# Gate and value products of a gated MLP as seven block products for each eight, with weight parts decoded early into DRAM

## The chip, the cores and the metric

One core of a Trainium2 chip runs the program. The metric is the device time of one execution in microseconds; lower is better. TensorE does the matrix products, VectorE (DVE in the rows), ScalarE (ACT) and GpSimd (POOL) the work on elements, and SyncE (SP) issues the DMAs.

## The reference

Three layers follow each other. The first is a linear attention with decay over 4 batches, 8 heads, 768 positions, in chunks of 32. Its output, 3072 tokens of 256, goes through an MLP with a cosine, and that through a gated MLP:

```python
h = x @ w_in
g = h * np.cos(h)
x = (g @ w_out).astype(np.float32)                  # d_ff 2048

gate = 1.0 / (1.0 + np.exp(-(x @ w_gate)))
val = x @ w_val
return (gate * val @ w_out).astype(np.float32)      # d_ff 1536, w_gate drawn 8 times larger
```

The weights arrive as 64-bit floats and are decoded on the chip.

## The kernel before, in words

Tokens are worked in NJ = 6 blocks j of 512 (128 positions of each of the 4 batches), held in `x2` with the 256 features as two halves of 128 partitions. Hidden units are worked in blocks f of 128: 16 in the cosine MLP, 12 in the gated one. Every product is made from split operands, a high part (`hi`, a rounded copy) and a low part (the rest): high x high, low weight x high data, high weight x low data.

The attention (`add_att`) and the cosine MLP (`add_mlp1`) of different blocks overlap. `add_conv1` decodes the cosine MLP's weights. When the last attention block is done, `open_later` gives its SBUF to the gated MLP's buffers, and `add_conv2` decodes that MLP's weights, one f at a time: three loads of 64-bit words (L323), then four instructions that make a 32-bit float in `wk` (L336 or L338 rebase, L343 shift, L347 low word, L353 sign), then a high copy (L299) and a low part (L304). They go into two buffers `own` and into the room of the cosine MLP's weights `w1` as that comes free.

The gated MLP (`add_mlp2`) has 72 steps, six blocks j of twelve f. A step has six matmuls of 512 columns for gate and six for value (`hid`, recorded under the helper's line L292), a sigmoid from PSUM on ScalarE (L777), gate times value on VectorE (L779), a high copy of the result (L299 or L301), a low part (L304), and the output product: four matmuls of 512 columns with the result's high part as weights and four of 256 with its low part. `add_split` makes the high and low parts of a block's tokens. Step s's output stands behind step s+1's gate and value products. After f = 11 the four output banks are evacuated (L299, L806) and written by SP (L809).

The order on every engine is fixed when the program is built. `add` records each operation with the engines it may use and their costs, and what it reads and writes; `Order.run` places operations one by one on the engine where each ends first, by due times that `rank` works back from the places (`turn`) that products have on TensorE. The constants in `P` set these (`t0`, `stretch`, `hop`, `slack` and others). `Shared` costs are those that the planner does not let overlap with POOL. So one changed cost or constant moves rows on all engines.

Of the kernel before, what the change touches and what calls it, by code (L numbers as in the profile page):

```python
# [8 lines left out]
F32 = mybir.dt.float32  # L9
# [21 lines left out]
    t0=30000,  # L31
    stretch=(1.2, 1.0),
    hop=500,
    gap=50,
    late=100,
    dlat=2500,
    slack=50,
    hid=-2.4,
    op1=1.3,
# [155 lines left out]
def linear_attention__then__cos_mlp__then__gated_mlp_kernel(  # L195
# [70 lines left out]
    r_t = ring(const, 2, [128, TOK], F32, "r")  # L266
    sq_t = ring(const, 2, [128, TOK], F32, "sq")
    gm_t = ring(const, 2, [128, TOK], F32, "gm")
    gh_t = ring(const, 2, [128, TOK], F32R, "gh")
    gl_t = ring(const, 2, [128, TOK], F32R, "gl")  # L270

    a_clip = [dram.tile([NB * H, S], F32, name=f"a_clip{i}") for i in range(2)]
# [38 lines left out]
    def add_conv(fs, srcs, raw, raw_r, wk, wk_r, hi_lo, w_r, extra=()):  # L311
# [13 lines left out]
        for f in fs:  # L325
            for i in range(len(srcs)):
                at = len(rows)
                rows.append(raw_r(at))
                add({"SP": 730}, lambda e, f=f, i=i, at=at: load(f, i, at), w=[rows[at]], r=extra)
# [57 lines left out]
    OWN = 2  # L387

    def w2_at(f):
        if f < OWN:  # L390
            return later["own"][f][:, 0], later["own"][f][:, 1]
        o = (f - OWN) * 768
        return w1[:, 0, o:o + 768], w1[:, 1, o:o + 768]

    def w2_out(f):
        if f < OWN:
            return later["own"][f][:, :, 512:768]
        o = (f - OWN) * 768
        return w1[:, :, o + 512:o + 768]

    def w2_room(f):
        return [("own", f)] if f < OWN else [("w1", 3 * (f - OWN) + i) for i in range(3)]

    NR = 4

    def add_conv2(f):
        add_conv(
            (f,), w2_src, lambda: later["raw"][f % NR], lambda at: ("raw", f % NR, at), lambda: later["wk"][f % 3],
            ("wk2", f % 3), lambda: w2_at(f), w2_room(f), extra=["later"],
        )  # L410
# [261 lines left out]
    def add_mlp1(s):  # L672
        j, f, first, last, again = steps[s]
        p, hb = xt_room(j), h_bank[s % 3]
        hp, u = bank[hb], s % 2
# [4 lines left out]
        def hid(e):  # L680
# [11 lines left out]
        r, sq, g, gh, gl = r_t[u], sq_t[u], gm_t[u], gh_t[u], gl_t[u]  # L692
        ri = r.bitcast(I32)
        hr = [("bank", hb)]
        add({"ACT": act_b(512) - 40}, lambda e: nc.scalar.activation(  # L695
            out=ri, in_=hp, func=ACTF.Identity, bias=quarter_sb), r=hr + ["round"], w=[("r", u)])
        add({"DVE": dve(512)}, lambda e: nc.vector.tensor_tensor(  # L697
            out=r, in0=ri, in1=hp, op=ALU.subtract), r=hr, w=[("r", u)])
        add({"ACT": act_b(512)}, lambda e: nc.scalar.activation(  # L699
            out=sq, in_=r, func=ACTF.Sin, scale=-TURN, bias=right_sb), r=[("r", u)], w=[("sq", u)])  # L700
        add({"DVE": dve(512)}, lambda e: nc.vector.tensor_tensor(  # L701
            out=g, in0=sq, in1=hp, op=ALU.mult), r=hr + [("sq", u)], w=[("gm", u)])
# [35 lines left out]
    TOTAL1 = NJ * FF1  # L740

    def slot2(s):
        return TOTAL1 + 2 + 1.5 * s

    def add_split(j):
        p = j % 2
        for k in range(KD):
            src, room = x2[:, j, k * TOK:(k + 1) * TOK], [(("x2", j), k)]
            xh = [("xh", p, b, k) for b in range(NB)]
            xl = [("xl", p, b, k) for b in range(NB)]  # L750
            add({"ACT": act(512), "DVE": dve2(512)}, lambda e, k=k, src=src: copy(e, xt_hi[p][:, k], src),
                r=room, w=xh)
            add({"POOL": pool(512), "DVE": dvs(512)},
                lambda e, k=k, src=src: minus(e, xt_lo[p][:, k], src, f32(xt_hi[p][:, k])), r=room + xh, w=xl)

    def add_mlp2(s):
        j, f = divmod(s, FF2)
        p, u = j % 2, s % 2
        gb, vb = gv_bank[s % 2]
        xh = [("xh", p, b, k) for b in range(NB) for k in range(KD)]  # L760
        xl = [("xl", p, b, k) for b in range(NB) for k in range(KD)]
        wh, wl = ([(n, *y) for y in w2_room(f)] for n in ("hi", "lo"))

        def hid(m, o):
            n = 0
            for i, xv in ((0, xt_hi), (1, xt_hi), (0, xt_lo)):
                for k in range(KD):
                    c = m * 256 + k * 128
                    mm(o, w2_at(f)[i][:, c:c + 128], xv[p][:, k], start=(n == 0), stop=(n == 3 * KD - 1))
                    n += 1  # L770

        shared = {5: ["cb"], 6: [("ya", 0), "ds"], 7: ["ct", ("ya", 1), ("turned", 0), ("turned", 1)]}
        for m, bk in enumerate((gb, vb)):
            add({"PE": 1362}, lambda e, m=m, bk=bk: hid(m, bank[bk]),
                r=xh + xl + wh + wl, w=[("bank", bk)] + shared.get(bk, []), turn=(slot2(s - 1) + 0.1 * m, 2))
        sg, g, gh, gl = sq_t[u], gm_t[u], gh_t[u], gl_t[u]
        add({"ACT": act(512)}, lambda e: nc.scalar.activation(  # L777
# [121 lines left out]
```

## Time and profile before

| | us |
|---|---|
| median of 3 runs (660.06 to 661.70) | 661.25 |
| profiled execution | 659.34 |
| span of its trace, first to last instruction | 657.6 |
| TensorE, matmuls busy | 627.8 (95%) |
| VectorE busy | 469.5 (71%) |
| ScalarE busy | 320.7 (49%) |
| POOL busy | 214.5 (33%) |

The span is the profiled execution less 1.74 us around it. Busy is the time in which an engine has an instruction under way; matmuls overlap, so one matmul's record is longer than the distance to the next. A wait stands beside the instruction that ended it.

### The profile page before, as it was taken

Reading aid. Unit: us, or ns where it says so; the run is one execution under the profiler, and the core shown is the slowest. Engines: PE = TensorE matmul, PEld = TensorE weight load, DVE = VectorE, ACT = ScalarE, POOL = GpSimd, SP = SyncE. Lnnn points to the kernel's source line nnn. Section 1 sums busy time; section 2 is a strip of 40 time slices with the busy share of each in tenths; the row PEclk is TensorE's granted clock in tenths of the full one; section 3 lists DMA queues with packets and bytes.
Section 4 is the critical chain, followed back from the end, with each engine's and each line's share of the span. In section 5 each row is a group of like instructions: output and inputs, shape, how many; then the busy total and the mean of one; then the engine's idle time right before and its main releaser. Section 6 shows DMA issues by size and latency. Waiting matters only on the chain.

```text
span 657.6 us, 9670 instructions
## 1 busy us (share of the span) xinstructions
PE 627.8 (95%) x3468; PEld 498.2 (76%) x3468; DVE 469.5 (71%) x810; ACT 320.7 (49%) x568; POOL 214.5 (33%) x206
## 2 busy tenths in 40 slices
PE   3678999999999999999999999999999999999997
PEld 2355688768867867877788888888888888888886
DVE  7999989997998698686889976446446446445444
ACT  3365799758767766754989632112112112112111
POOL 2336777758767557644565000000000000000000
PEclk9999999999999999999999999999999999999999
DMA  8999950566397167123424200000000000000100
GB/s 161 195 218 232 206 119 27 128 120 114 76 177 157 37 119 138 33 40 99 154 90 140 97 0 14 20 0 10 23 1 8 25 1 3 31 1 0 33 1 32
DMA packets 158947, 50.67 MB, mean 77 GB/s; under 512 B 118515, under 2 KB 155219, under 8 KB 158899
## 3 DMA queue, kind: packets, MB, share of 16 engines
q1 hardware_dynamic: 158899, 50.05, 34.1%
q8 instruction: 27, 0.44, 0.3%
q14 instruction: 21, 0.17, 0.1%
HBM read 36.21 MB, written 3.34 MB: 60 GB/s over the span
## 4 chain that ended last, share of the span: by engine, by line
PE 85%; DVE 9%; DMA 2%; issue 2%; SPq 1%; ACT 0%; DVEq 0%
PE bank L292 85%; DVE lt L556 2%; DVE gm L701 1%; DVE g L573 1%; DVE r L697 1%; DMA raw<-in_moe_w_gate_dram 1%; SPq L323 1%; DVE wk L353 1%; DMA bc<-in_B_dram 1%; DMA x<-in_moe_w_out_dram 1%; DVE ee L535 1%; DMA ab<-in_a_dram 1%; DVE wk L343 1%; DVE xt_lo L637 0%; PE bank L532 0%
## 5 line engine op out<-in xcount | busy, mean ns | idle before, releaser
L292 PE MATMUL bank<-xt_hi,w 128*128 128x512 f32 x864 | 236.7, 395 | 2.6 <-DVE gm L701 1.8
L292 PEld LDWEIGHTS bank<-xt_hi,w 128*128 128x128 f32 x864 | 156.9, 189 | 33.7 <-DVE gm L701 2.8
L304 POOL TENSOR_TENSOR gl<-gm,gh 128x512 fp32r<-128x512 f32 x96 | 147.4, 1537 | 97.1 <-ACT gh L299 61.0
L777 ACT ACTIVATE sq<-bank 128x512 f32<-128x512 f32 x72 | 43.1, 598 | 210.6 <-PE bank L292 210.4
L779 DVE TENSOR_TENSOR gm<-sq,bank 128x512 f32<-128x512 f32 x72 | 49.5, 688 | 132.7 <-PE bank L292 131.2
L292 PE MATMUL bank<-xt_lo,w 128*128 128x512 f32 x432 | 133.6, 390 | 0.0
L292 PE MATMUL bank<-gh,w 128*128 128x512 f32 x384 | 107.4, 397 | 0.5 <-DVE x L731 0.5
L292 PEld LDWEIGHTS bank<-xt_lo,w 128*128 128x128 f32 x432 | 81.4, 188 | 17.8 <-DVE xt_lo L637 0.2
L695 ACT ACTIVATE r<-bank,quarter_sb 128x512 int32<-128x512 f32 x96 | 65.5, 683 | 36.9 <-PE bank L292 36.6
L292 PEld LDWEIGHTS bank<-gh,w 128*128 128x128 f32 x384 | 70.1, 188 | 17.3 <-ACT sq L699 1.1
L701 DVE TENSOR_TENSOR gm<-sq,bank 128x512 f32<-128x512 f32 x96 | 65.1, 679 | 24.2 <-ACT sq L699 22.5
L299 ACT ACTIVATE gh<-gm 128x512 fp32r<-128x512 f32 x103 | 64.8, 629 | 24.8 <-DVE gm L701 13.5
L699 ACT ACTIVATE sq<-r,right_sb 128x512 f32<-128x512 f32 x96 | 68.7, 718 | 8.0 <-DVE r L697 7.8
L697 DVE TENSOR_TENSOR r<-r,bank 128x512 f32<-128x512 int32 x96 | 65.0, 679 | 10.3 <-ACT r L695 9.6
L292 PE MATMUL bank<-w,gh 128*128 128x512 f32 x240 | 64.6, 389 | 0.0
L292 PE MATMUL bank<-gl,w 128*128 128x512 f32 x192 | 62.7, 401 | 0.0
L556 DVE TENSOR_TENSOR_SCAN lt<-ab,id_t 128x512 f32<-128x512 f32 x40 | 52.5, 1313 | 0.0
L292 PEld LDWEIGHTS bank<-w,gh 128*128 128x128 f32 x240 | 45.0, 188 | 9.2
L304 DVE TENSOR_TENSOR gl<-gm,gh 128x512 fp32r<-128x512 f32 x72 | 49.7, 691 | 2.1
L292 PEld LDWEIGHTS bank<-w,gl 128*128 128x128 f32 x240 | 36.8, 189 | 4.9 <-DVE gl L304 0.3
L292 PEld LDWEIGHTS bank<-gl,w 128*128 128x128 f32 x192 | 34.5, 188 | 7.4 <-issue 0.2
L292 PE MATMUL bank<-w,gl 128*128 128x256 f32 x240 | 38.7, 282 | 0.0
(98 smaller groups left out, 606.0 us busy)
## 6 DMA issues: line engine op xcount, KB each, us to landing
ab<-a_clip SPq DMA_DIRECT2D x20, 512.0 KB
x<-in_moe_w_in_dram SPq DMA_DIRECT2D x16, 256.0 KB
x<-in_moe_w_out_dram SPq DMA_DIRECT2D x16, 256.0 KB
xs<-in_x_dram SPq DMA_DIRECT2D x24, 128.0 KB
raw<-in_moe_w_gate_dram SPq DMA_DIRECT2D x12, 256.0 KB
raw<-in_moe_w_val_dram SPq DMA_DIRECT2D x12, 256.0 KB
raw<-in_moe_w_out_dram SPq DMA_DIRECT2D x12, 256.0 KB
out_dram<-o SPq DMA_DIRECT2D x24, 128.0 KB
```

Of the source, the lines that this page charges most:

```text
L292: nc.tensor.matmul(out_, lhsT, rhs, start=start, stop=stop, skip_group_check=True)
L299: nc.scalar.activation(out=out_, in_=in_, func=ACTF.Copy)
L304: engine[eng].tensor_tensor(out=out_, in0=in0, in1=in1, op=ALU.subtract)
L323: nc.sync.dma_start(out=dst, in_=src)
L343: nc.vector.tensor_scalar(out=wi, in0=wi, scalar1=3, scalar2=None, op0=ALU.logical_shift_left)
L556: add({"DVE": scan(512) if j else float(scan(512))}, lambda e, hs=hs, src=src: nc.vector.tensor_tensor_scan(out=lt[:, hs].rearrange("p h t ...
L695: add({"ACT": act_b(512) - 40}, lambda e: nc.scalar.activation(out=ri, in_=hp, func=ACTF.Identity, bias=quarter_sb), r=hr + ["round"], w=[ ...
L697: add({"DVE": dve(512)}, lambda e: nc.vector.tensor_tensor(out=r, in0=ri, in1=hp, op=ALU.subtract), r=hr, w=[("r", u)])
L699: add({"ACT": act_b(512)}, lambda e: nc.scalar.activation(out=sq, in_=r, func=ACTF.Sin, scale=-TURN, bias=right_sb), r=[("r", u)], w=[("sq ...
L701: add({"DVE": dve(512)}, lambda e: nc.vector.tensor_tensor(out=g, in0=sq, in1=hp, op=ALU.mult), r=hr + [("sq", u)], w=[("gm", u)])
L777: add({"ACT": act(512)}, lambda e: nc.scalar.activation(out=sg, in_=bank[gb], func=ACTF.Sigmoid), r=[("bank", gb)], w=[("sq", u)])
L779: add({"DVE": dve(512)}, lambda e: nc.vector.tensor_tensor(out=g, in0=sg, in1=bank[vb], op=ALU.mult), r=[("sq", u), ("bank", vb)], w=[("gm ...
```

## The change

Tokens of two blocks j and hidden units of two blocks f now form a pair. Its gate product is a 2 by 2 block matrix (features by hidden units) times a 2 by 2 block matrix (features by tokens), and so is its value product. Eight block products would make it; the change makes it with seven, after Strassen and Winograd. Four of the seven weight blocks are sums or differences (L488 in the new numbering), formed once and kept, so that a weight part has seven blocks; the seven token operands (`add_operands`) are formed once for two j. Four PSUM banks collect the seven products, and what two results share is moved between banks: twice a product set a bank is copied to SBUF on ScalarE (`put`) and added to two banks on VectorE, from PSUM and SBUF into PSUM (`plus`, L938). The sigmoid, the multiplication, the split and the output then run for the four results. The output product is turned to 256 columns throughout.

There are 18 pairs, six for each of three passes over two token blocks. The weights come in 18 parts (six double blocks, for gate, value and output), each of 256 by 256. The first six parts are decoded during the attention, into work buffers of the cosine MLP's decoding, and written to DRAM (`kept`); they are read back when the gated MLP's buffers are opened. The cosine MLP's four rings of intermediate results become one ring of three buffers, used in place.

```diff
 P = dict(
-    t0=30000,
-    stretch=(1.2, 1.0),
-    hop=500,
+    t0=18000,
+    stretch=(1.25, 1.0),
+    hop=700,
...
-    op1=1.3,
+    op1=1.0,
+    both=12,
+    early=6,
...
-    r_t = ring(const, 2, [128, TOK], F32, "r")
-    sq_t = ring(const, 2, [128, TOK], F32, "sq")
...
+    NG = 3
+    gm_t = ring(const, NG, [128, TOK], F32, "gm")
...
+    def add_early(n, p):
+        i = 3 * n + p
+        j = NJ - 1 - (i % 2 if i < P["both"] else 0)
+        wk, wk_r = wk1_t[i % 2][:, 0:512], ("wk1", i % 2)
+        add_decode(n, p, x2[:, j], [(("x2", j), k) for k in range(2)], lambda: wk, wk_r)
+        add({"SP": 700}, lambda e: nc.sync.dma_start(out=kept[i], in_=wk), r=[wk_r], w=[("kept", i)])
+
+    def add_conv2(n, p):
...
+        if i < P["early"]:
+            add({"SP": 700}, lambda e: nc.sync.dma_start(out=wk()[:, 0:512], in_=kept[i]),
+                r=["later", ("kept", i)], w=[wk_r])
+        else:
+            j = i % 2
+            add_decode(n, p, x2[:, j], [(("x2", j), k) for k in range(2)], lambda: wk()[:, 0:512], wk_r, ["later"])
+        if p < 2:
...
+            for o, x0, x1, op in ((4, 0, 2, ALU.add), (5, 4, 1, ALU.subtract), (6, 1, 0, ALU.subtract),
+                                  (7, 3, 5, ALU.subtract)):
+                add({"DVE": dvs(128), "POOL": pool(128)}, lambda e, o=o, x0=x0, x1=x1, op=op: engine[e].tensor_tensor(
+                    out=block(o), in0=block(x0), in1=block(x1), op=op), w=[wk_r])
...
-    def add_mlp2(s):
-        j, f = divmod(s, FF2)
...
+    P6, P1, P5, P2, P3, P7, P4 = (4, 0), (0, 1), (3, 2), (2, 3), (6, 4), (5, 5), (1, 6)
+    own_op = {5: ("xh", 2), 2: ("xl", 2), 0: ("xh", 0), 1: ("xl", 0), 6: ("xh", 1)}
...
+        b11, b12, b21, b22 = half(j0, 0), half(j1, 0), half(j0, 1), half(j1, 1)
...
+        less(tt, b22, b12, rb22 + rb12, t)
+        split(5, tt, t)
+        less(b12, b12, b11, rb11, rb12)
+        split(2, b12, rb12)
...
+    def add_pair(n):
+        jp, fp = divmod(n, NP)
...
+            product(P6, be, True, 0.1)
+            product(P1, al, True, 0.2)
+            put(0, al)
+            plus(de, be, 0)
+            plus(be, be, 0)
+            product(P5, ga, True, 0.3)
+            out_before(2 * m)
+            product(P2, al, False, 1.1)
+            product(P3, de, False, 1.2)
+            product(P7, be, False, 1.3)
+            put(1, ga)
+            plus(de, de, 1)
+            plus(ga, be, 1)
+            out_before(2 * m + 1)
+            product(P4, be, False, 2.1)
```

Each `product` is three matmuls of 512 columns. `be`, `al`, `ga`, `de` are the four banks, which change roles from one product set to the next.

How rows move is shown at three places. TensorE in the last pass, one whole step before; `bank0` to `bank7` are PSUM banks, `xt_hi`/`xt_lo` the tokens' parts, `w1` weights, `gh`/`gl` the results' high and low parts:

```order
L292 MATMUL bank1_67<-xt_hi1_84,w1_82 128x512 x4
L292 MATMUL bank1_67<-xt_lo1_87,w1_82 128x512 x2
L292 MATMUL bank2_68<-xt_hi1_84,w1_82 128x512 x4
L292 MATMUL bank2_68<-xt_lo1_87,w1_82 128x512 x2
L292 MATMUL bank3_69<-w1_82,gh0_95 128x512
L292 MATMUL bank4_70<-w1_82,gh0_95 128x512
L292 MATMUL bank5_71<-w1_82,gh0_95 128x512
L292 MATMUL bank6_72<-w1_82,gh0_95 128x512
L292 MATMUL bank3_69<-w1_82,gl0_97 128x256
L292 MATMUL bank4_70<-w1_82,gl0_97 128x256
L292 MATMUL bank5_71<-w1_82,gl0_97 128x256
L292 MATMUL bank6_72<-w1_82,gl0_97 128x256
```

and now, from the first product set's P1 of a pair to behind its P3 (`xt` and `op` buffers hold the seven token operands; `xt_lo1` holds the fourth result's parts):

```order
L294 MATMUL bank0_66<-xt_lo0_86,w1_82 128x512 x3
L294 MATMUL bank5_71<-xt_hi0_83,w1_82 128x512 x3
L294 MATMUL bank3_69<-w1_82,xt_lo1_87 128x256 x2
L294 MATMUL bank4_70<-w1_82,xt_lo1_87 128x256 x2
L294 MATMUL bank2_68<-xt_lo2_88,w1_82 128x512 x3
L294 MATMUL bank3_69<-w1_82,gh0_92 128x256 x2
L294 MATMUL bank4_70<-w1_82,gh0_92 128x256 x2
L294 MATMUL bank3_69<-w1_82,gh0_92 128x256 x2
L294 MATMUL bank4_70<-w1_82,gh0_92 128x256 x2
L294 MATMUL bank1_67<-op1_2917,w1_82 128x512 x3
L294 MATMUL bank3_69<-w1_82,gl0_95 128x256 x2
L294 MATMUL bank4_70<-w1_82,gl0_95 128x256 x2
```

Products of three and short output runs of four or eight matmuls alternate; the output is that of the pair before.

VectorE where the gated MLP begins, before (`L701` and `L697` belong to the cosine MLP, the others decode):

```order
L347 SCALAR_TENSOR_TENSOR wk20_2852<-raw3_2851,wk20_2852 128x768
L697 TENSOR_TENSOR r1_90<-r1_90,bank1_67 128x512
L353 SCALAR_TENSOR_TENSOR wk20_2852<-raw3_2851,wk20_2852 128x768
L697 TENSOR_TENSOR r0_89<-r0_89,bank2_68 128x512
L701 TENSOR_TENSOR gm1_94<-sq1_92,bank1_67 128x512
L343 TENSOR_SCALAR wk21_2853<-wk21_2853 128x768
L304 TENSOR_TENSOR w1_82<-wk20_2852,w1_82 128x768
```

and now, in its first pass (`L938` are the new additions, `L966` gate times value, `L306` low parts, `L451` a decode):

```order
L938 TENSOR_TENSOR bank5_71<-bank0_66,cp0_2918 128x512
L966 TENSOR_TENSOR gm0_89<-gm0_89,bank1_67 128x512
L938 TENSOR_TENSOR bank0_66<-bank0_66,cp0_2918 128x512
L938 TENSOR_TENSOR bank5_71<-bank5_71,cp1_2919 128x512
L451 SCALAR_TENSOR_TENSOR wk20_2914<-x2_81,wk20_2914 128x512
L966 TENSOR_TENSOR gm1_90<-gm1_90,bank5_71 128x512
L938 TENSOR_TENSOR bank2_68<-bank0_66,cp1_2919 128x512
L306 TENSOR_TENSOR gl0_95<-gm0_89,gh0_92 128x512
L966 TENSOR_TENSOR gm2_91<-gm2_91,bank2_68 128x512
L306 TENSOR_TENSOR gl1_96<-gm1_90,gh1_93 128x512
L966 TENSOR_TENSOR gm3_2920<-gm3_2920,bank0_66 128x512
L306 TENSOR_TENSOR w1_82<-wk21_2915,w1_82 128x896
```

The additions that TensorE's products wait for stand in one queue with decodes and low parts. SP during the attention's last blocks (`stk`, `bc`, `xs`, `ab` are the attention's inputs), now:

```order
L428 DMA x2_81<-in_moe2_w_gate_dram 128x2x256
L465 DMA kept1_144<-wk11_142 128x512
L428 DMA x2_81<-in_moe2_w_out_dram 128x2x256
L465 DMA kept0_143<-wk10_141 128x512
L613 DMA_TRANSPOSE stk1_120<-pk1_116 128x16x128
L513 DMA xs3_104<-in_x_dram 128x8x32
L513 DMA bc0_105<-in_C_dram 128x8x16
```

Before, no weight load and no store stood between the attention's rows there.

## Rows read from the trace of the kernel before

**Rows 1.** The page, busy us, share of the span and count of each engine.

```profile
PE 627.8 (95%) x3468; PEld 498.2 (76%) x3468; DVE 469.5 (71%) x810; ACT 320.7 (49%) x568; POOL 214.5 (33%) x206
```

**Rows 2.** Windows: busy us (count) of PE, PEld, DVE, ACT, POOL; clock, DMA share, GB/s.

```profile
0.00:66.00 66.00, 43.08 (x351) 26.49 (x352) 60.68 (x123) 32.10 (x67) 25.27 (x33) 1.00 0.97 201
...
200.00:306.00 106.00, 105.98 (x677) 80.91 (x670) 84.88 (x157) 72.46 (x126) 60.26 (x56) 1.00 0.39 76
...
356.00:400.00 44.00, 44.00 (x213) 37.05 (x213) 36.14 (x53) 22.38 (x32) 1.63 (x1) 1.00 0.17 55
400.00:640.00 240.00, 240.00 (x1165) 202.38 (x1164) 117.47 (x208) 43.28 (x82) 0.00 (x0) 1.00 0.04 12
```

**Rows 3.** Chain of waits, late part: start us, length us, what.

```profile
308.86 4.30 DMA raw<-in_moe_w_gate_dram
...
318.05 334.48 PE bank L292 x1601
...
652.97 1.47 DVE o L806 x4
```

**Rows 4.** Timeline of TensorE, one gated step: start us, length us, instructions.

```profile
500.44 1.07 PE L292 MATMUL bank<-xt_hi,w 128*128 128x512 f32 x4
501.34 0.62 PE L292 MATMUL bank<-xt_lo,w 128*128 128x512 f32 x2
...
502.70 0.64 PE L292 MATMUL bank<-w,gl 128*128 128x256 f32 x4
503.17 1.09 PE L292 MATMUL bank<-xt_hi,own 128*128 128x512 f32 x4
504.10 0.62 PE L292 MATMUL bank<-xt_lo,own 128*128 128x512 f32 x2
504.56 1.07 PE L292 MATMUL bank<-xt_hi,own 128*128 128x512 f32 x4
```

**Rows 5.** Timeline of VectorE in the same stretch.

```profile
503.01 0.42 DVE L301 CAST gh<-gm 128x512 fp32r<-128x512 f32 x1
503.34 0.68 DVE L304 TENSOR_TENSOR xt_lo<-x,xt_hi 128x512 fp32r<-128x512 f32 x1
503.94 0.68 DVE L304 TENSOR_TENSOR gl<-gm,gh 128x512 fp32r<-128x512 f32 x1
```

**Rows 6.** Groups by line and shape: count, busy us, mean ns, idle before.

```profile
L779 DVE TENSOR_TENSOR gm<-sq,bank 128x512 f32<-128x512 f32 x72 | 49.5, 688 | 132.7 <-PE bank L292 131.2 <-POOL gl L304 1.2 <-ACT wk L336 0.3
L292 PEld LDWEIGHTS bank<-w,gl 128*128 128x128 f32 x240 | 36.8, 189 | 4.9 <-DVE gl L304 0.3
L301 DVE CAST gh<-gm 128x512 fp32r<-128x512 f32 x65 | 27.7, 426 | 2.1
L347 DVE SCALAR_TENSOR_TENSOR wk<-raw,wk 128x768 int32<-128x768 int32 x12 | 12.7, 1060 | 0.0
L561 POOL TENSOR_TENSOR bd<-bc,lt 128x128 f32<-128x128 f32 x16 | 8.6, 540 | 5.9 <-DVE lt L556 3.2 <-PE bank L292 2.6
L304 POOL TENSOR_TENSOR own<-wk,own 128x768 fp32r<-128x768 f32 x1 | 1.9, 1866 | 0.1
L561 DVE TENSOR_TENSOR bd<-bc,lt 128x128 f32<-128x128 f32 x4 | 1.1, 281 | 0.0
```

**Rows 7.** The same view, VectorE alone, 356 to 402 us.

```profile
L347 DVE SCALAR_TENSOR_TENSOR wk<-raw,wk 128x768 int32<-128x768 int32 x6 | 5.7, 950 | 0.0
```

**Rows 8.** Timeline of POOL from 333 us.

```profile
333.38 1.87 POOL L304 TENSOR_TENSOR gl<-gm,gh 128x512 fp32r<-128x512 f32 x1 [0.72 <-ACT gh L299]
336.16 1.29 POOL L304 TENSOR_TENSOR gl<-gm,gh 128x512 fp32r<-128x512 f32 x1 [0.90 <-ACT gh L299]
```

**Rows 9.** Waits of the queue of SP: us in total, times, longest.

```profile
SPq L526 <- DVE pk L304: 21.3, 2, 19.0
```

More of the change, by code (lines that the diff above doesn't have):

```diff
@@ L304, in minus, with add_conv @@
         engine[eng].tensor_tensor(out=out_, in0=in0, in1=in1, op=ALU.subtract)
-    def add_conv(fs, srcs, raw, raw_r, wk, wk_r, hi_lo, w_r, extra=()):
+    def add_conv(fs, srcs, raw, raw_r, wk, wk_r, hi_lo, w_r):
         n = 256 * len(srcs) * len(fs)
@@ L328, in add_conv @@
                 rows.append(raw_r(at))
-                add({"SP": 730}, lambda e, f=f, i=i, at=at: load(f, i, at), w=[rows[at]], r=extra)
+                add({"SP": 730}, lambda e, f=f, i=i, at=at: load(f, i, at), w=[rows[at]])
         def words(i):
@@ L383, in add_conv1 @@
         )
[L387 to L410, printed above, removed]
+    NP = FF2 // 2
+    W_COLS = (7 * 128, 7 * 128, 2 * DM)
+    W_FROM = (0, 7 * 128, 14 * 128)
+    PAIR = 14 * 128 + 2 * DM
+    def w2_part(n, p):
+        if n == NP - 1 and p == 1:
+            o = 3 * PAIR
+            return w1[:, :, o:o + W_COLS[p]]
+        if 2 <= n < 5:
+            o = (n - 2) * PAIR + W_FROM[p]
+            return w1[:, :, o:o + W_COLS[p]]
+        o = W_FROM[p] if n < 2 else (0, 0, W_COLS[0])[p]
+        return later["own"][n % 3][:, :, o:o + W_COLS[p]]
@@ new lines, in linear_attention__then__cos_mlp__then__gated_mlp_kernel, with g_of, g_room @@
+    parts = [0, 1, 2, 5]
+    bank_r = {0: [("bank", 0)], 1: [("bank", 1)], 2: [("bank", 2)], 5: ["cb"], 3: [("bank", 3)], 4: [("bank", 4)],
+              6: [("ya", 0), "ds"], 7: ["ct", ("ya", 1), ("turned", 0), ("turned", 1)]}
+    y2_bank = ((3, 4), (6, 7))
+    def g_of(kind, i):
+        if i < NG:
+            return {"gm": gm_t, "gh": gh_t, "gl": gl_t}[kind][i]
+        return later["gm"] if kind == "gm" else xt_lo[1][:, ("gh", "gl").index(kind)]
+    def g_room(kind, i):
+        if i < NG or kind == "gm":
+            return [(kind, i)]
+        return [("xl", 1, b, ("gh", "gl").index(kind)) for b in range(NB)]
@@ L813, in open_later @@
+    NW = 2
     def open_later(e):
@@ L841, in linear_attention__then__cos_mlp__then__gated_mlp_kernel @@
         add_conv1(n, f, cuts[n + 1])
+    for n in range(NP):
+        for p in range(3):
+            if 3 * n + p < P["early"]:
+                add_early(n, p)
     for s, step in enumerate(steps):
@@ L853, in linear_attention__then__cos_mlp__then__gated_mlp_kernel @@
     add({"NONE": 0}, open_later, w=att_rooms + ["later"])
-    for f in range(FF2):
-        add_conv2(f)
-    for j in range(NJ):
-        add_split(j)
-        for s in range(j * FF2, (j + 1) * FF2):
-            add_mlp2(s)
+    add_operands(0)
+    for n in range(NP):
+        for p in range(3):
+            add_conv2(n, p)
+    for n in range(NP * NJ // 2):
+        if n % NP == 0 and n:
+            add_operands(n // NP)
+        add_pair(n)
     with tc.manual_schedule():
```

239 lines of the change are left out of this document (161 added, 78 removed).

## The prediction

> **What bounds the kernel now.** I read the page first: TensorE is busy 95% of the span [rows 1]. The windows by stage say where the other 5% lie: 22.9 us of TensorE's idle time fall into the first 66 us, and from 400 to 640 us TensorE is busy 240.00 of 240.00 us at a granted clock of 1.00 [rows 2]. The chain of waits agrees: it runs from 318.05 us for 334.48 us through 1,601 matmuls without a step on another engine, and only the last output lies behind it [rows 3]. So the gated MLP costs what its matmuls cost. The timeline shows one step of it, start to start: from 500.44 to 504.56 us, 4.12 us [rows 4]; 72 steps make 296.6 us. In the same stretch VectorE is busy 117.47 of 240 us and POOL not at all, while from 356 to 400 us, where the weights are still decoded, VectorE is busy 36.14 of 44 us [rows 2].
>
> **The change, part by part.** The sum is made against the profiled execution, 659.34 us, 1.91 us under the median of the three runs, 661.25 us.
>
> *A, products.* Two token blocks and two hidden blocks now form a pair; 18 pairs replace 72 steps. Four steps had 48 gate and value matmuls of 512 columns; a pair has 2 x 7 x 3 = 42. The output had 16 of 512 and 16 of 256 columns and now has 48 of 256, the same columns. A matmul of 512 takes (501.34 - 500.44)/4 = 0.225 us, one of 256 (503.17 - 502.70)/4 = 0.1175 us, and the first four behind a run of 256s take 0.93 in place of 0.90 us [rows 4]. A pair has about nine such runs: 42 x 0.225 + 48 x 0.1175 + 9 x 0.03 = 9.45 + 5.64 + 0.27 = 15.36 us; 18 pairs are 276.5 us, so **A = -20.1 us**. Without the 0.03 it is 15.09 us and -25.0; with all that a step has beyond 16 x 0.225 put on its four short matmuls, 0.13 us each, it is 15.69 us and -14.2.
>
> *B, VectorE in the first of three passes.* A pair adds eight PSUM additions on VectorE and four copies on ScalarE, and the first pass (six pairs, 92.2 us of TensorE) also decodes twelve of the eighteen weight parts and forms their extra blocks. No row shows an addition that writes PSUM; the nearest reads PSUM and writes SBUF in 688 ns [rows 6]. From the first such addition to the last of pair six the order holds 158 VectorE instructions: 124 of 512 columns at one rate, 6 of 896, 9 of 128, and 19 copies or one-input operations of 512. Start to start, 512 columns take 503.94 - 503.34 = 0.60 us and a cast 0.33 [rows 5]; 896 is estimated from 768 columns at 950 ns [rows 7] as 1.11 us, less the same 0.09 of overlap, and 128 takes 281 ns [rows 6]. That is 74.4 + 6.1 + 2.5 + 6.3 = 89.3 us. At the full durations, 688 and 426 ns [rows 6], it is 85.3 + 6.7 + 2.5 + 8.1 = 102.6 us; many of these instructions follow in place on the one before, which cannot overlap. I take the middle, 96 us: VectorE then ends the pass, and **B = +3.8 us**, from 0 (all hidden under TensorE) to +10.4. What is late next is the weight part of the following pair, and behind its product stands everything on TensorE.
>
> *C, the other passes and their seams.* Here VectorE has 109 instructions a pass, 96 of them at 0.60 to 0.688 us, 62 to 72 of 92.2 us: load is no bound, latency may be. Between the end of a pair's seventh product (P7 of the value half) and the third product of the next pair, VectorE has nine instructions in order: the last addition, four gate multiplications, three low halves, and the sum that this third product adds onto; 9 x 0.60 = 5.4 us, 6.2 at 0.688. TensorE has five products and 24 short matmuls for the same time, 5 x 3 x 0.225 + 24 x 0.1175 = 6.2 us. That leaves 0 to 0.8 us for the hand-overs between the engines, so a wait of 0.1 us a pair is my middle, 12 x 0.1 = 1.2 us. The seven operands are single-buffered; at the last seam their eleven instructions bring two pairs to some 29 us of VectorE's time against 30.7 of TensorE's, with 0.8 us more for what comes late there. **C = +2 us**, from 0 (all hidden) to +8 (one instruction late, 0.6 us, in each of twelve pairs, and the seam).
>
> *D, the end.* The last output still needs evacuation and a write. Behind the last product TensorE has 32 short matmuls, 3.8 us, over the last gate chain (multiply, cast, subtract: 0.688 + 0.426 + 0.688 = 1.8 us [rows 6], and lags). **D = +0.5 us**, from 0 to +2.
>
> *E, up to the gated MLP.* Six decodes move ahead of the attention's last block: 6 x (2 x 0.688 + 2 x 0.426) = 13.4 us on VectorE [rows 6], or less where ScalarE rebases. VectorE has 106 - 84.88 = 21.1 us idle there while TensorE has 0.02 [rows 2], so I cost them at nothing; without that cover they cost up to 13.4. The queue of SP gets 6 stores and 6 loads of 256 KB, and 36 loads of 256 KB become 18 of double size; the DMA engines are 39% busy there [rows 2]. The chain cos-MLP on one ring of three buffers in place of three rings of two, and the other constants of the planner, move rows all through this part. TensorE's 0.02 us of idle leaves nothing to win behind 200 us; the first 66 us can go either way, and I bound that by a fifth of their 22.9 idle us. **E = +1 us**, from -4 to +5.
>
> The sum: -20.1 + 3.8 + 2 + 0.5 + 1 = -12.8 us; 646.5 us for the profiled execution, and with 1.91 us **648 us for the median**. With the terms' ends combined as independent, about 10 us either way, this case's own range is 639 to 658.
>
> **One rule against the change.** A POOL subtraction of 512 columns takes 1.29 us in one row and 1.87 us in another of the same stretch [rows 8], and VectorE's 768-column decode takes 1060 ns over all twelve, 950 ns where POOL had one instruction in 44 us [rows 2, 6, 7]: the two engines slow each other by some tenths. The Trainium skill, page "SBUF — State Buffer", section "Who interferes with whom", says that GpSimd and a VectorE instruction with two SBUF inputs share one port pair as an exclusive lock, and the loser blocks for the whole instruction. By that rule the first pass, with POOL and VectorE on the same work buffers, would lose about what the second rival below gives; the trace bears out the direction, not yet that size.
>
> **The rivals.**
> 1. *All hidden.* Additions, decodes and operands fit under TensorE: B and C are 0, E is -1 to 0. For it: in the stage from 356 us VectorE is 82% busy and TensorE never waits [rows 2]. Against it: the first pass asks 97 to 111% of VectorE. It gives 661.25 - 20 = 641 us, 637 at the lower bound of A. Chance 0.20.
> 2. *POOL and VectorE exclude each other in the first pass (slower).* POOL's list there has 18 block sums at 540 ns, two subtractions of 896 at 1866 x 896/768 = 2.18 us [rows 6] and seven of 512 at 1.29 to 1.87 us [rows 8]: about 9.7 + 4.4 + 10 = 24 us. If VectorE stands still through all of it, the pass takes 96 + 24 = 120 us, 27.8 over TensorE's 92.2, and the run 648 + 24 = 672 us. It decides from about 109 us of VectorE's time in that pass; there the forecast's gain of 13 us is eaten. For it: the longer rows above. Against it: 72 of the 158 VectorE instructions have an operand in PSUM, and the losses seen are 0.1 to 0.6 us. Chance 0.10.
> 3. *SP's stores hold up the attention.* A store of a decoded part waits in SP's order until VectorE is done, and the last block's transposes and B, C, x loads stand behind it. A load of half the size took 4.30 us [rows 3] and a decode 2.2: 6.5 us each, three of the six stores have attention rows behind them, 19.6 us if nothing covers it. For half of it: a transpose already waited 19.0 us for VectorE without TensorE noticing [rows 9]. 648 + 10 = 658 us. Chance 0.12.
> 4. *Short matmuls run at the weight load.* Each 256-column matmul has its own load, 189 ns in the records [rows 6]; at that pace a pair takes 9.45 + 48 x 0.189 = 18.5 us, more than the four steps' 16.5, and the product saved would be no saving: 661.25 + 18 x 2 and the other terms, some 706 us. Against it: four in a row went at 0.1175 us [rows 4]. Chance 0.03.
>
> **How the numbers follow.** The forecast has 0.52, the rivals 0.20, 0.10, 0.12 and 0.03, and 0.03 are for what I do not see. The range, 637 to 661 us, holds the forecast's own, the first rival and the third, and leaves out the second, the fourth and the tails. A measurement here tells about 0.3% from no change, 2 us: faster is under 659.3, slower above 663.2. Faster: nearly all of 0.52, 0.20, somewhat over half of 0.12, a little of the rest, 0.79. Slower: 0.10, 0.03 and scraps, 0.14. Same: 0.07.
>
> **What would show it.** A: 18 pairs at 15.1 to 15.7 us, read as the distance between equal products in the last pass. B: TensorE's waits on VectorE gather in the 92 us behind the first gated product, on additions or on weight parts, 4 us in all, with VectorE over 95% busy. C: short waits of some tenths once a pair. E: TensorE without gaps from 200 us on to the first gated product, which starts at most 5 us later than now. I am wrong if a pair without waits is over 16 us, if the first pass loses more than 10 us, or if gaps appear between 200 and 306 us.

## The result, and the profile after

The changed kernel takes **644.31 us**, median of 4 runs (643.51 to 644.87), against 661.21 us (660.06 to 661.70) for the kernel before on the same chip: ratio 0.9746, interval 0.9729 to 0.9763, 16.9 us faster. The prediction was 648 us, 637 to 661, faster with 0.79.

The profiled execution took 643.51 us, its span is 641.7 us, 15.9 less than before.

| term | forecast, us | measured, us | read from |
|---|---|---|---|
| A, products | -20.1 (a pair 15.36) | -19.8 (a pair 15.38) | distance of equal products, last pass: 18 x 15.38 = 276.8 against 296.6 |
| B, first pass, and C, later passes | +3.8 and +2 | +0.5 together | TensorE's waits from 345 us on |
| D, the end | +0.5 | +1.8 | last matmul to the end of the span, 5.8 us against 4.0 |
| E, up to the gated MLP | +1 | +1.6 | what is left of -15.9 |

The page of the changed kernel, busy us of each engine, to be held against [rows 1]:

```profile
PE 612.0 (95%) x3648; PEld 495.3 (77%) x3648; DVE 541.8 (84%) x924; ACT 395.9 (62%) x711; POOL 246.2 (38%) x255
```

TensorE lost 15.8 us of work, about what the span lost. VectorE gained 72 us, ScalarE 75. The windows by stage, columns as in [rows 2] (the last three are TensorE's granted clock, DMA share and GB/s):

```profile
0.00:66.00 66.00, 43.90 (x336) 27.46 (x337) 59.96 (x118) 32.45 (x68) 24.72 (x36) 0.85 0.97 206
...
200.00:306.00 106.00, 105.83 (x664) 79.63 (x664) 95.83 (x173) 73.74 (x133) 61.37 (x56) 1.00 0.51 108
345.00:440.00 95.00, 94.78 (x518) 82.07 (x517) 92.57 (x156) 60.68 (x100) 33.04 (x37) 1.00 0.18 56
440.00:535.00 95.00, 94.74 (x555) 83.41 (x554) 73.34 (x121) 42.55 (x76) 7.16 (x6) 1.00 0.04 12
535.00:630.00 95.00, 94.99 (x562) 83.94 (x561) 64.56 (x106) 44.72 (x81) 2.11 (x2) 1.00 0.04 12
```

The early decodes stand where they were forecast: VectorE has 95.83 us from 200 to 306 us, 10.95 more than before [rows 2], and TensorE loses 0.17 there. In the first pass (345 to 440 us) VectorE is busy 97%, and TensorE works 94.78 of 95 us all the same. All that TensorE waits for from 345 us to the end of the span is this (wait, us in total, times, longest):

```profile
PE bank L294 <- DVE gm L966: 0.3, 1, 0.3
PE bank L294 <- DVE bank L938: 0.2, 1, 0.2
```

VectorE's timeline in the first pass (start us, length us) shows at what pace its full queue runs:

```profile
433.04 0.69 DVE L938 TENSOR_TENSOR bank<-bank,cp 128x512 f32<-128x512 f32 x1
433.64 0.41 DVE L442 TENSOR_SCALAR wk<-wk 128x512 int32<-128x512 int32 x1
434.09 0.69 DVE L446 SCALAR_TENSOR_TENSOR wk<-x,wk 128x512 int32<-128x512 int32 x1
434.70 0.69 DVE L938 TENSOR_TENSOR bank<-bank,cp 128x512 f32<-128x512 f32 x1
435.30 0.68 DVE L451 SCALAR_TENSOR_TENSOR wk<-x,wk 128x512 int32<-128x512 int32 x1
```

An addition from PSUM into PSUM has a record of 0.69 us, as estimated from [rows 6], but the next instruction starts 0.60 us behind it. Instructions that go on in place mostly have an addition between them; where they follow directly, as the second decode step on the shift, they stand 0.45 instead of 0.33 us apart. The forecast's 158 instructions are those from the first addition of the pass to just before the first one of the next pass:

```profile
353.57 1.30 DVE L938 TENSOR_TENSOR bank<-bank,cp 128x512 f32<-128x512 f32 x2 [0.26 <-PE bank L294]
354.78 1.47 DVE L451 SCALAR_TENSOR_TENSOR wk<-x,wk 128x512 int32<-128x512 int32 x1
...
449.82 0.70 DVE L938 TENSOR_TENSOR bank<-bank,cp 128x512 f32<-128x512 f32 x1
```

That is 96.25 us, where the forecast had 89.3 to 102.6 and took 96. Of the 7.0 us over the lower end, 3.4 us are six instructions that ran beside one of POOL's and took longer than others of their kind (the decode step at 354.78 is one), and for 2.1 us VectorE is idle; where the other 1.5 us lie stays open.

TensorE waits for only 0.2 us in this stretch because it has as much to do itself: 282 matmuls of 512 columns and 260 of 256, which is 94.0 us at 0.225 and 0.1175 us, with the changes between them to be added. 23 of the 282 are output products of the cosine MLP (`gh` or `gl` before `w`), which still stand among the first pairs' products:

```profile
353.37 1.07 PE L294 MATMUL bank<-gh,w 128*128 128x512 f32 x4
...
368.82 0.39 PE L294 MATMUL bank<-gl,w 128*128 128x512 f32 x1
```

### The profile page after: what moved, and what is told of

Its sections match the earlier page's. It is cut to its first block, busy times and chain, and to the rows that moved or that the text cites. A ratio compares the mean times of both kernels' runs of the same rounds, so it can differ in the third digit from the quotient of the medians.

```text
span 641.7 us, 10229 instructions
## 1 busy us (share of the span) xinstructions
PE 612.0 (95%) x3648; PEld 495.3 (77%) x3648; DVE 541.8 (84%) x924; ACT 395.9 (62%) x711; POOL 246.2 (38%) x255
## 4 chain that ended last, share of the span: by engine, by line
PE 88%; DVE 6%; SPq 2%; issue 1%; DMA 1%; ACT 1%; POOL 0%; ACTq 0%; DVEq 0%
PE bank L294 87%; DVE lt L643 1%; DMA x<-in_moe_w_out_dram 1%; SPq L513 1%; DVE wk L349 1%; DVE gm L784 1%; DVE gm L788 1%; DVE bank L938 1%; PE bank L619 0%; SPq L325 0%; ACT wk L338 0%; DVE wk L345 0%; DVE g L660 0%; DVE g L672 0%; DVE wk L355 0%
## 5 line engine op out<-in xcount | busy, mean ns | idle before, releaser
L306 POOL TENSOR_TENSOR gl<-gm,gh 128x512 fp32r<-128x512 f32 x102 | 148.7, 1463 | 146.7 <-ACT gh L301 108.4
L294 PE MATMUL bank<-xt_hi,w 128*128 128x512 f32 x573 | 160.0, 399 | 2.0 <-DVE xt_hi L721 1.0
L938 DVE TENSOR_TENSOR bank<-bank,cp 128x512 f32<-128x512 f32 x144 | 97.3, 694 | 47.4 <-PE bank L294 38.6
L294 PEld LDWEIGHTS bank<-xt_hi,w 128*128 128x128 f32 x573 | 104.9, 190 | 24.6 <-ACT xt_hi L720 1.1
L294 PE MATMUL bank<-xt_lo,w 128*128 128x512 f32 x318 | 94.3, 392 | 0.0
L782 ACT ACTIVATE gm<-bank,quarter_sb 128x512 int32<-128x512 f32 x96 | 65.5, 683 | 29.7 <-PE bank L294 24.9
L786 ACT ACTIVATE gm<-gm,right_sb 128x512 f32<-128x512 f32 x96 | 68.8, 719 | 12.9 <-DVE gm L784 12.1
L784 DVE TENSOR_TENSOR gm<-gm,bank 128x512 f32<-128x512 int32 x96 | 64.7, 678 | 12.5 <-ACT gm L782 12.1
L788 DVE TENSOR_TENSOR gm<-gm,bank 128x512 f32<-128x512 f32 x96 | 64.8, 678 | 9.9 <-ACT gm L786 9.6
L963 ACT ACTIVATE gm<-bank 128x512 f32<-128x512 f32 x72 | 41.9, 598 | 48.1 <-DVE bank L938 32.5
L301 ACT ACTIVATE cp<-bank 128x512 f32<-128x512 f32 x72 | 43.1, 598 | 33.8 <-PE bank L294 32.0
L966 DVE TENSOR_TENSOR gm<-gm,bank 128x512 f32<-128x512 f32 x72 | 47.3, 680 | 1.6 <-PE bank L294 1.3
L306 DVE TENSOR_TENSOR gl<-gm,gh 128x512 fp32r<-128x512 f32 x48 | 33.5, 707 | 0.3 <-ACT gh L301 0.2
```

What stands on the lines that cost most here:

```text
L294: nc.tensor.matmul(out_, lhsT, rhs, start=start, stop=stop, skip_group_check=True)
L301: nc.scalar.activation(out=out_, in_=in_, func=ACTF.Copy)
L306: engine[eng].tensor_tensor(out=out_, in0=in0, in1=in1, op=ALU.subtract)
L784: add({"DVE": dve(512)}, lambda e: nc.vector.tensor_tensor(out=g, in0=ri, in1=hp, op=ALU.subtract), r=hr, w=[("gm", u)])
L786: add({"ACT": act_b(512)}, lambda e: nc.scalar.activation(out=g, in_=g, func=ACTF.Sin, scale=-TURN, bias=right_sb), w=[("gm", u)])
L788: add({"DVE": dve(512)}, lambda e: nc.vector.tensor_tensor(out=g, in0=g, in1=hp, op=ALU.mult), r=hr, w=[("gm", u)])
```

## The experiments

All edits are to the changed kernel unless said otherwise, and times are held against its 644.31 us. In the second and third group instructions were only inserted: every other row of every engine kept its place. The runs came in three series, in which the kernel before took 660.26 to 660.90 us beside its 661.21 here, so a difference of a us or less says nothing.

**1. Eight products in the same pairs.**

```diff
-            product(P6, be, True, 0.1)
-            product(P1, al, True, 0.2)
-            put(0, al)
-            plus(de, be, 0)
...
+            product((1, 1), al, True, 0.1)
+            product((3, 3), al, False, 0.2)
+            product((1, 2), de, True, 0.3)
+            out_before(2 * m)
...
+            product((0, 1), be, True, 2.1)
+            product((2, 3), be, False, 2.2)
```

> The changed kernel with eight block products in place of seven: same pairs, same decoding, same output products, but plain token blocks and plain weight blocks, no sums of blocks, no copies and additions between banks. Theory (the matmul count alone sets the pair): 48 x 0.225 + 48 x 0.1175 + 9 x 0.03 = 16.7 us a pair against 15.38 in the changed kernel, 18 pairs +24 us, so 668 us, slower than the kernel before by about 1%: the split of the output into short matmuls costs 4 us that only the saved product pays back. Rival (the additions and sums cost TensorE something that its gaps do not show, in longer matmuls or at the seams): leaving them out gives part of it back, 664 us or less.

Measured: **669.68 us** (669.41 to 669.91), 25.4 more, the theory; 1.0137 of the kernel before (1.0119 to 1.0156). Two equal places one pair apart, from TensorE's timeline, first with eight products, then with seven:

```profile
588.03 0.64 PE L294 MATMUL bank<-own,xt_lo 128*128 128x256 f32 x4
...
604.82 0.64 PE L294 MATMUL bank<-own,xt_lo 128*128 128x256 f32 x4
```

```profile
577.04 0.64 PE L294 MATMUL bank<-own,gl 128*128 128x256 f32 x4
577.51 0.86 PE L294 MATMUL bank<-xt_lo,w 128*128 128x512 f32 x3
...
592.89 0.86 PE L294 MATMUL bank<-xt_lo,w 128*128 128x512 f32 x3
```

604.82 - 588.03 = 16.79 us against 592.89 - 577.51 = 15.38; 18 times 1.41 is 25.4. So the saved product is worth what its six matmuls take, and the additions cost TensorE nothing that can be seen: VectorE had only 62.34 us in the first pass here, and TensorE gained nothing by it. Without the saving the pairs alone are slower than the kernel before.

**2. More VectorE work, inserted.** Subtractions of 512 columns into a buffer that nothing reads, in the first pass (`n < NP`), in the later passes (`n >= NP`), and there at a second place too (`plus(be, be, 0, 3 if m == 1 else 0)`):

```diff
+            def spare(eng, k):
+                for _ in range(k if n < NP else 0):
+                    eng.tensor_tensor(out=later["dum"], in0=id_t[:, 32:544], in1=id_t[:, 32:544], op=ALU.subtract)
...
-                    out=bank[to], in0=bank[x], in1=later["cp"][i], op=ALU.add), r=bank_r[x][:1] + [("cp", i)], w=bank_r[to])
+                    out=bank[to], in0=bank[x], in1=later["cp"][i], op=ALU.add), spare(nc.vector, k)), r=bank_r[x][:1] + [("cp", i)], w=bank_r[to])
...
-            plus(ga, be, 1)
+            plus(ga, be, 1, 3 if m == 0 else 0)
```

> The changed kernel with three more VectorE subtractions of 512 columns in each pair of the first pass (18 in all, behind the last addition of the gate half, into a buffer that nothing reads; the order of everything else is untouched). Theory (that pass is at the edge): 18 x 0.60 = 10.8 us against 2.4 us in which VectorE is idle there, so +8 us, 652; at 0.69 us each +10, 654. Rival (what looks like a full VectorE is partly instructions that wait their turn at no cost to TensorE): under +3 us, 647 or less.

> The changed kernel with six more VectorE subtractions of 512 columns in each pair of the second and third pass (72 in all, three behind the last addition of the gate half and three behind the second addition of the value half, into a buffer that nothing reads; nothing else moved). Theory (load is no bound there and the additions have time to spare): 72 x 0.60 = 43 us against 52 us of VectorE's idle time in the two passes, 0 to +3 us, 644 to 647. Rival (the chain of additions, multiplications and low parts is tight, as term C of the prediction had it: each trio of 1.8 us is late by more than the spare 0 to 0.8 us): 24 trios by about 1 us, 668 us.

> The changed kernel with three more VectorE subtractions of 512 columns in each pair of the second and third pass, behind the last addition of the gate half (36 in all, into a buffer that nothing reads): the same trio as in the run on the first pass, twice as many of them, where VectorE is 68 to 77% busy. Theory (what counts is how full VectorE's queue is, and the run with six a pair lost its 12 us because that took VectorE to 90% and because of the trio in the value half): 36 x 0.60 = 21.6 us find room, 0 to +3 us, 644 to 647. Rival (the chain of the gate half is tight by itself; any 1.8 us there costs TensorE about half a us, as 12 us over 24 trios say): 12 x 0.5 = +6 us, 650.

Measured: 18 in the first pass, **654.66 us** (652.89 to 655.62), +10.3, the theory at its upper end. 36 in the later passes, **646.47 us** (646.09 to 648.31), +2.2, the theory. 72 there at two places, **656.26 us** (655.41 to 656.38), +12.0. TensorE's waits from 300 us on and the first pass, for the 18:

```profile
PE bank L294 <- DVE bank L942: 7.0, 6, 1.7
PE bank L294 <- ACT cp L301: 0.7, 1, 0.7
PE bank L294 <- DVE gm L970: 0.3, 1, 0.3
```

```profile
345.00:440.00 95.00, 88.01 (x467) 73.79 (x466) 93.14 (x155) 56.65 (x93) 33.03 (x36) 1.00 0.17 56
```

In the first pass there is no room: VectorE's busy time stays at 93 of 95 us and everything moves back by what was inserted, 18 x 0.60 = 10.8 us. In the later passes twice as many cost a fifth of that. The run with six a pair fell between its theory and the rival. The twelve trios in the value half are the difference between the last two of these, 9.8 us, 0.8 us for each trio of 1.8; so the chain of the value half has about 1 us to spare, as worked out from this difference, and that of the gate half nearly all of 1.8 us. That it is the chain and not a fuller VectorE is argued, not shown: no run has the trios of the value half alone.

**3. More POOL and more ScalarE work, inserted.** Three of either in each pair of the first pass, and six POOL subtractions in each pair of the later ones, behind the first gate multiplication of a pair:

```diff
+                for k in range(3 if i == 0 and n < NP else 0):
+                    nc.gpsimd.tensor_tensor(out=later["dum"], in0=id_t[:, 32:544] if k else g_of("gm", 0),
+                                            in1=id_t[:, 32:544], op=ALU.subtract)
```

> The changed kernel with three more POOL subtractions of 512 columns in each pair of the first pass (18 in all, the counterpart of the 18 VectorE subtractions that cost 10 us there). Theory (tenths at most, though here VectorE has no room, so each tenth shows): 18 x 0.1 to 0.3 = +2 to +5 us, 646 to 649. Rival (VectorE stands still for them whenever it has two SBUF operands, about half of its time there): 18 x 1.3 to 1.9 by a half, +12 to +17 us, 656 to 661. No effect at all: 644.

> The changed kernel with three more ScalarE copies of 512 columns in each pair of the first pass (18 in all, placed as the 18 POOL subtractions were, into a buffer that nothing reads). Theory (POOL's 18 cost 10 us because POOL and VectorE get in each other's way on SBUF, about half a us each; ScalarE has 34 of 95 us to spare and does not touch VectorE's pace): 18 x 0.6 = 11 us find room, 0 to +2 us, 644 to 646, VectorE's low parts stay near 0.77 us. Rival (any engine's extra work delays VectorE's inputs or its memory): +5 us or more, 649.

> The changed kernel with six more POOL subtractions of 512 columns in each pair of the second and third pass (72 in all, the first reads a result of the pair, so they run spread over the pairs; into a buffer that nothing reads; nothing else moved). At 1.29 us each POOL is busy 7.7 of 15.4 us there. Theory (POOL and VectorE slow each other by tenths at most, the second rival of the prediction is wrong): VectorE's low parts go from 0.68 to 0.8 us or so, 0 to +3 us, 644 to 647. Rival (VectorE stands still for a whole POOL subtraction whenever it has two SBUF operands): up to four low parts a pair late by 1.3 to 1.9 us each, 5 to 7 us on top of 12 of 15.4, so 2 to 4 us a pair, +24 to +48 us, 668 to 692.

Measured: 18 on POOL in the first pass, **654.27 us** (653.71 to 654.59), +10.0, between theory and rival. 18 on ScalarE there, **649.95 us** (649.02 to 650.44), +5.6: the rival. 72 on POOL later, **669.95 us** (669.01 to 671.44), +25.6: the rival's range by its number, but not by its mechanism alone. Groups of VectorE by line and shape from 470 to 640 us in this last run, where the changed kernel has 696, 683, 680 and 425 ns for the same four:

```profile
L943 DVE TENSOR_TENSOR bank<-bank,cp 128x512 f32<-128x512 f32 x78 | 52.0, 693 | 47.3 <-PE bank L294 40.1 <-ACT gm L968 7.1
L306 DVE TENSOR_TENSOR gl<-gm,gh 128x512 fp32r<-128x512 f32 x27 | 27.8, 1039 | 0.2 <-ACT gh L301 0.2
L971 DVE TENSOR_TENSOR gm<-gm,bank 128x512 f32<-128x512 f32 x40 | 25.9, 679 | 0.8 <-PE bank L294 0.7
...
L303 DVE CAST gh<-gm 128x512 fp32r<-128x512 f32 x6 | 4.5, 753 | 0.5 <-PE bank L294 0.3
```

The two groups with an operand in PSUM keep their time; those that work in SBUF alone get longer by a half or more. A single pair from the timeline:

```profile
571.08 1.61 POOL L939 TENSOR_TENSOR dum<-gm,id_t 128x512 f32<-128x512 f32 x1 [14.86 <-DVE gm L971]
...
571.46 1.52 DVE L303 CAST gh<-gm 128x512 fp32r<-128x512 f32 x1
```

The cast, 0.43 us elsewhere, ends 0.29 us behind POOL's instruction. That is the rule of the Trainium skill, page "SBUF — State Buffer", section "Who interferes with whom": one port pair, one holder at a time, for which a VectorE instruction with two inputs in SBUF contends, or a cast in a mode that uses both ports, and one with at most one input in SBUF otherwise not. The trace agrees, 693 and 679 ns beside 1039 and 753. In the first pass the low parts `gl` of VectorE go from 772 to 1131 ns by POOL's 18, and to 854 by ScalarE's. In the run with 72 the time is not that of the shared ports alone. TensorE's waits from 440 us on there:

```profile
PE bank L294 <- DVE bank L943: 6.5, 7, 1.3
PE bank L294 <- POOL op L306: 5.1, 1, 5.1
PE bank L294 <- POOL gl L306: 4.2, 1, 4.2
PE bank L294 <- DVE gm L971: 0.3, 1, 0.3
```

9.3 us are two results of POOL's own that stood in its queue behind six inserted instructions, an effect of where they were put. And the copies on ScalarE, which left VectorE's decodes at their pace (L451 750 ns, 752 without them), cost 5.6 us because the casts of the gate chain stood behind them; VectorE, full as it is, had to stop for them (waits of VectorE, 350 to 445 us):

```profile
DVE gl L306 <- ACT gh L301: 2.5, 3, 1.2
DVE wk L442 <- ACT wk L435: 0.7, 1, 0.7
```

So POOL does lengthen VectorE's work in SBUF, and in the first pass any engine that holds up VectorE costs time. How much is whose can be worked out from the timelines of the same 158 instructions, 96.25 us in the changed kernel. With POOL's 18 they take 106.9 us: 21 of them, each beside one of POOL's, are 13.5 us longer than others of their kind, against six and 3.4 us, and VectorE is idle for 3.0 us against 2.1. So the 10.0 us are nearly all such lengthening. The group with the most of it:

```profile
L306 DVE TENSOR_TENSOR gl<-gm,gh 128x512 fp32r<-128x512 f32 x12 | 13.5, 1131 | 1.7 <-ACT gh L301 1.7
```

With ScalarE's 18 they take 102.4 us: 4.7 us more are idle, and 1.4 us more are lengthening.

**4. The order: parts decoded early, and the planner's constants.** No part early (`early=0`), nine (`early=9`), the changed kernel with the constants of before, and the kernel before with the new ones:

```diff
-    t0=18000,
-    stretch=(1.25, 1.0),
-    hop=700,
+    t0=30000,
+    stretch=(1.2, 1.0),
+    hop=500,
...
```

> The changed kernel with no part decoded early: all 18 are decoded behind the opening of the gated MLP's buffers, most of them in the first pass. Theory (VectorE is full there, 92.6 of 95 us): the 11 us that VectorE had more between 200 and 306 us come back into the pass, 103.5 of 95 us, so 8 to 11 us of waits of TensorE on VectorE, and at the opening up to 6 us more for the first part's load (3.6 us) and decode; 653 to 661 us. Rival (the planner finds room on POOL, 33 of 95 us busy, and ScalarE): waits under 3 us, 644 to 647 us.

> The changed kernel with nine parts decoded early instead of six. Theory (TensorE waits 0.5 us in the first pass as it is, so 5.5 us of room for VectorE there buys at most that): 643.5 to 646 us, the more if three more stores and decodes in the attention's last blocks hold something up. Rival (a pass at its edge loses small amounts everywhere, so that room gives back 2 us or more): under 642.5, which would beat both kernels.

> The changed kernel with the planner's constants of the kernel before (t0, stretch, hop, late, dlat, slack, op1). Theory (the gain is the saved product's and the constants only move rows in the shade of TensorE): 643 to 647 us. Rival (a first pass in which VectorE is 97% busy fits only with an order made for it; with shorter hand-over times in the plan, additions stand too late): waits of TensorE on additions in the first pass, 649 us or more.

> The kernel before with the planner's constants of the changed kernel, nothing else. Theory (as above): 659 to 663 us, no change. Rival (part of the measured gain is the constants'): under 657 us. What it tells besides: whether the lower clock of TensorE in the first 66 us (granted clock 0.85 in the changed kernel, 1.00 before) comes with the constants.

Measured: no part early **653.21 us** (652.60 to 654.59), +8.9; nine early **651.44 us**, median of three runs (650.21 to 651.85; a fourth took 1202.85, which nothing here explains), +7.1, outside theory and rival; old constants **652.59 us** (650.06 to 653.03), +8.3, the rival; the kernel before with new constants **663.34 us** (662.28 to 663.66), 1.0045 of itself (1.0031 to 1.0060), 3.0 more than in its own series, so the rival is out. The first pass, of no part early, old constants and nine early:

```profile
345.00:440.00 95.00, 89.72 (x481) 75.61 (x480) 91.70 (x160) 59.26 (x98) 27.36 (x30) 1.00 0.20 67
```

```profile
345.00:440.00 95.00, 91.40 (x493) 78.23 (x492) 90.06 (x157) 59.56 (x97) 26.81 (x29) 0.98 0.18 59
```

```profile
345.00:440.00 95.00, 92.20 (x499) 78.80 (x498) 88.72 (x150) 62.16 (x102) 31.77 (x34) 1.00 0.21 64
```

With nine parts early VectorE has less to do there, yet it stands idle 6.3 us and TensorE loses 2.8, against 2.4 and 0.2 in the changed kernel. So the 8.9 us of the first run can't be put down to six decodes more alone, though the number fell in the theory's range: each of the three edits gives the planner another order, and each other order loses 7 to 9 us. Of these 7.0, 6.5 and 4.5 us (no part early, old constants, nine early) are waits of TensorE from 345 us on, none over 1.8 us, on additions, multiplications, casts and sigmoids; the rest stays open. With no part early they are:

```profile
PE bank L294 <- DVE bank L938: 4.1, 3, 1.7
PE bank L294 <- DVE gh L303: 1.9, 2, 1.4
PE bank L294 <- ACT gm L963: 0.7, 1, 0.7
PE bank L294 <- DVE w L306: 0.3, 1, 0.3
```

The changed kernel's order is one that fits a full VectorE, and constants and early parts are a part of that. On the kernel before, which has room in the gated MLP, the same constants cost 3 us, none of it there: TensorE has no wait from 345 us on.

**5. The end.** The last two token blocks by four copies of 512 columns and four writes of 256 KB:

```diff
-                    out=out[b * S + j * T:b * S + (j + 1) * T, :], in_=dst), r=room)
+                    out=out.rearrange("(b s) d -> s b d", b=NB)[j * T:(j + 1) * T, b - 1:b + 1, :],
+                    in_=dst2.rearrange("p (b d) -> p b d", b=2)), r=room)
```

> The changed kernel with its last two token blocks evacuated by four copies of 512 columns (two on ScalarE, two on VectorE) instead of eight of 256 (six on ScalarE), and written by four DMAs of 256 KB instead of eight of 128 KB. Theory (the end is set by eight DMA issues in a row, 3.77 us, behind six copies in a row, 1.91 us): the last issue ends near 637.6 in place of 639.5 us and a larger write lands somewhat later, -0.5 to -2 us, 642.3 to 643.8. Rival (the landing of the last bytes sets the end, whatever the number of issues): no change, 644.3.

Measured: **644.14 us** (642.28 to 644.64), the rival: no difference that can be told from none (0.9755 of before, 0.9734 to 0.9776). The end of the timeline of SP, of the changed kernel and of this run:

```profile
635.73 3.77 SPq L914 DMA_DIRECT2D out_dram<-x  x8
```

```profile
636.74 1.98 SPq L924 DMA_DIRECT2D out_dram<-x  x4
```

The issues got shorter by 1.8 us, as expected, and the span still ends 3.6 us behind the last issue (642.3 us) instead of 2.2 (641.7): the larger writes land later, 2.7 us by the median against 1.8. From the last matmul to the end it is 5.6 instead of 5.8 us.

## Why the prediction was right, and where it was off

**A** held, to 0.02 us a pair, and the run with eight products shows that it is the whole gain: 25.4 us measured for what 18 x 6 matmuls of 0.225 us, 24.3, should be. The 0.03 us for a change between matmuls of 512 and 256 columns held too. The fourth rival, short matmuls at the pace of their weight loads, is out: four of them take 577.51 - 577.04 = 0.47 us.

**B** came out too large, with the right cost of VectorE held against the wrong time of TensorE. The step that failed is "VectorE then ends the pass", 96 us against "92.2 us of TensorE". VectorE's 158 instructions took 96.25 us, but TensorE had work for nearly all of that time: the 92.2 us are six pairs alone, while 5.2 us of the cosine MLP's output (23 matmuls of 0.225) stand among the first of them, and most of the sixth pair's output falls behind the stretch. That the middle was met to 0.3 us is luck in part. It was to cover instructions in place that can't overlap; those cost some 0.1 us each, and the order rarely lets them follow directly. What filled it are the 3.4 us beside POOL and 2.1 us of idle time. That the pass is at its edge was right all the same: 18 more instructions cost 10.3 us, and the forecast's 3.8 lies between this order's waits of 0.5 and the 4.5 to 7.0 us of the three other orders.

**C** was too large as well: "a wait of 0.1 us a pair" did not come, and "0 to 0.8 us for the hand-overs" is about 1 us in the value half by the runs with inserted subtractions, and more in the gate half, so nothing waits. Of TensorE's two waits the one on a multiplication, 0.3 us, stands at the seam of the first and second pass; the other, 0.2 us, belongs to the first pass.

**D** was too small: a copy and a write were counted for the last output, but two token blocks end together, so eight writes follow the last matmul where four did before. That their number sets the time is not borne out: with four writes of twice the size the end is 5.6 us.

**E** came out at 1.6 for 1, as what the other terms leave, and no store of SP's holds TensorE up: between 100 and 345 us it has one wait, 0.2 us. What the 1.6 us consist of is not shown; the new constants, which cost the kernel before 3 us ahead of its gated MLP, may be it. The third rival, stores that hold up the attention, is out.

The first rival, all hidden, at 0.20, was nearer to B and C than the forecast; with D and E as measured it would have given the result. The second, POOL against VectorE, is a real mechanism with a small price here: in the first pass of the changed kernel `gl` takes 772 ns against 683 later (13 times), the last decode step 752 against 682 for the step before it (11 times), a sum of blocks 446 against the 281 of [rows 6] (9 times): 1.2 + 0.8 + 1.5, with rounding 3.4 us of VectorE's time instead of the rival's 24. It stands in six instructions alone, each beside one of POOL's: one decode step took 1.47 us, the ten others 0.68. 72 of the 158 instructions have an operand in PSUM, and POOL has 33 us of work in the 95. But the price grows with POOL's work: 18 more of its instructions made it 13.5 us.

The errors, -5.3 in B and C, +1.3 in D, +0.6 in E and +0.3 in A, add up to the 3.1 us by which the span fell further (15.9) than forecast (12.8).

## What to carry to other kernels

Where TensorE is the bound all the time, price a saved product by the start-to-start time of its matmuls, and then count what the additions ask of the fullest stage of each helping engine, at start-to-start times, with what a neighbour on the same memory adds. Hold that against all that the bound engine does in the same stretch, what is left of the layer before too, and not against the new products alone. An engine that is 97% full can be hidden, but then the time hangs on the order: three small edits of the order, one of which even took work off that engine, cost 7 to 9 us. Before adding work to a stage, insert some idle copies of it there and see what they cost; it showed room for nearly all of 36 instructions in one stage and for none of 18 in another.

## What the runs showed of the hardware

TensorE's granted clock, 1.00 in every window of the profiled execution before, fell in the first 66 us of the changed kernel's. The windows there:

```profile
24.00:26.00 2.00, 0.36 (x3) 0.17 (x5) 2.00 (x5) 0.58 (x2) 1.95 (x3) 0.94 1.11 275
26.00:38.00 12.00, 8.81 (x71) 5.43 (x70) 11.55 (x26) 4.04 (x9) 2.56 (x5) 0.50 1.01 214
38.00:40.00 2.00, 2.00 (x9) 1.34 (x7) 2.00 (x3) 0.86 (x3) 0.84 (x2) 0.64 1.21 209
```

0.50 is the lower of its two levels, 1.2 GHz, and it comes after 2 us in which TensorE worked 0.36. With the old constants the first 66 us are at 1.00, and the kernel before with the new ones has 0.89 there. But the order alone does not decide it: in the run with 18 POOL subtractions, which has the changed kernel's order up to its first pass, the clock is 1.00 from 26 to 38 us, behind 2 us with 0.78 us of matmuls. Nor does it cost time that can be seen, with TensorE idle for 22 of the first 66 us: the four executions of the changed kernel had a mean clock of 0.983, 0.994, 0.976 and 0.994 and took 643.51, 644.49, 644.87 and 644.12 us. Where TensorE is the bound it does cost. In the run with 72 POOL subtractions a wait of 5.1 us did the same in the middle of the gated MLP: 550 to 556 us, with 1.18 us of matmuls, then 4 us at half the clock, in which eight matmuls of 256 columns took 558.57 - 556.87 = 1.70 us instead of 8 x 0.1175 = 0.94. So such a wait costs more than its length.

```profile
550.00:556.00 6.00, 1.18 (x8) 0.70 (x6) 1.87 (x3) 0.81 (x2) 5.76 (x5) 0.85 0.00 0
556.00:560.00 4.00, 3.73 (x13) 3.35 (x14) 1.89 (x3) 0.60 (x1) 0.22 (x1) 0.50 0.00 0
```

```profile
556.27 0.79 PE L294 MATMUL bank<-op,own 128*128 128x512 f32 x1 [5.09 <-POOL op L306]
556.87 1.91 PE L294 MATMUL bank<-own,gh 128*128 128x256 f32 x8
558.57 1.48 PE L294 MATMUL bank<-xt_hi,own 128*128 128x512 f32 x3
```
